# Four 32-column TensorE tiles for the softmax sums and value products of a fused attention and SwiGLU kernel

## The chip, the cores and the metric

The kernel runs on one core of one Trainium2 chip. The metric is the device time of one execution in microseconds (us). A profile of one execution gives the span of the instructions on the core, which is a little shorter than the time of the run.

## The reference

Eight batches of eight heads, 576 positions, 64 channels: causal attention over a sliding window of 64 positions. Its result, with the heads side by side (512 features for each of 4608 tokens), goes through a SwiGLU block with 1536 hidden features.

```python
scores = scale * np.matmul(q, k.transpose(0, 1, 3, 2))
mask = (rel >= 0) & (rel < window)          # window = 64
scores = np.where(mask, scores, -1000000000.0)
attn = np.exp(scores - np.max(scores, axis=-1, keepdims=True))
attn = attn / (np.sum(attn, axis=-1, keepdims=True) + 1e-09)
attn_out = np.matmul(attn, v)
...
x = attn_out.transpose(0, 2, 1, 3).reshape(B * S, H * D)
g = x @ w_gate
out = (g / (1.0 + np.exp(-g)) * (x @ w_val)) @ w_out
```

## The kernel before

The 4608 tokens are worked in nine groups `t` of 512. Groups 0 to 6 and group 8 are the first 512 positions of one batch each; group `LAST` (7) holds the last 64 positions of all eight batches. Within a group everything lies transposed: features on the 128 partitions, the 512 tokens along the free dimension. Heads are taken in four pairs `u`; head `2u` uses partitions 0 to 63 and head `2u+1` partitions 64 to 127.

For one group, `scores(t, u)` multiplies keys and queries block by block on 64x64 tiles of TensorE, ScalarE (ACT) takes the exponential of a two-bank PSUM tile into the weights `E`, and from group 1 on VectorE (DVE) multiplies `E` with a mask. Keys lie on the partitions of `E`, 128 of them as two blocks of 64. `totals` (L251) multiplies `E` with ones to get the softmax sums, copied onto the 64 partitions of each head: one 512-column matmul per head on a 128x64 tile. ACT takes the logarithm of the sums (`log`, L259) and the exponential of its negative (`invert`, L262), which gives the inverse. `mix` (L275) multiplies the values with `E`: for each of eight 64-token blocks `m` and each head of the pair one matmul of 64 stationary columns (the channels of `v1` or of `v2`, a copy of `v1` shifted by 64 positions) and 64 moving columns. `scale` (L285) multiplies the result by the inverse into `xT`, chunk `u` of four. PSUM tiles for scores, wide sums and products come from `ps_a` (two tiles of two banks); those for gates, outputs and single sums from `ps_f` (tags `g` and `v`, two banks each).

Then come twelve `gate_value` steps `m` (L332), each with four matmuls of `xT` with `wg` and four with `wv`, a Silu on ACT (L325) and a product on DVE (L326) into `hT`. `project` (L341) multiplies `hT` with `wo`, twelve matmuls for each quarter `s` of the group's tokens; its output is copied by `project_end` and stored.

The order on each engine is that of the program text; nothing is rescheduled. From group 2 on a group's attention runs between the four projections of the group before: scores of pairs 0 and 1, `project(t-1, 0)`, scores of pairs 2 and 3, sums of pairs 0 and 1, `project` 1 and 2, sums of pairs 2 and 3, all products (`mix_all`), `project(t-1, 3)`, and then the twelve gate steps, in which the next group's queries and keys are turned by DVE.

The start is written out by hand. Queries, keys and half the values of group 0 come over the SP and ACT queues as float32; they are cast by ACT, DVE and POOL (GpSimd) as the table `casts` says (L450) and turned on TensorE (`turn_pe`). Filler matmuls (`keep_warm`, L411) stand between. POOL issues, in this order, the other half of the values of group 0, `wg` and `wv` in column ranges (`weights_gv`, L166), the keys of group 1 (`k_r`, L73), the last range of `wg` and `wv`, the queries of group 1 (`q_s`, L87), two thirds of `wo` (L172), the values of group 1 (L128) and the last third of `wo`. POOL's issue of a transfer waits, with eight under way, for the one eight issues back to land. Gate steps 0 and 1 of group 0 are interleaved with the products of pairs 2 and 3 (`gate_part`, L312). During gate steps 5 to 9 the keys of group 1 are joined by ACT and turned on TensorE (L180); DVE turns its queries (`turn_q`, L192) from step 9 on. Group 0's projection is done for all four quarters at once, in chunks `columns(c0, c1)` of `hT` between group 1's scores, sums and products.

Of the kernel before, what the change touches and what calls it, by code (L numbers as in the profile page):

```python
# [17 lines left out]
def kernel(  # L18
# [131 lines left out]
    def shift_pair(t, u):  # L150
        hs = slice(2 * u, 2 * u + 2)
        a, b = v1[t % 2][:, :, hs], v2[t % 2][:, :, hs]
        nc.vector.tensor_copy(b[64:128, 1:4], a[64:128, 0:3])
        nc.vector.tensor_copy(b[0:64], a[0:64])
# [9 lines left out]
    def weights_gv(f0, f1, c0=0, c1=4):  # L164
        for src, dst in ((moe_w_gate, wg), (moe_w_val, wv)):
            nc.gpsimd.dma_start(  # L166
                dst[:, c0:c1, f0:f1],
                src[P * c0:P * c1, f0:f1].rearrange("(c r) f -> r c f", r=P),
            )
# [79 lines left out]
    def totals(t, u, d_ps):  # L249
        for h in range(2):  # L250
            nc.tensor.matmul(  # L251
                d_ps[64 * h:64 * h + 64], ones[:, 0:D], weights[t, u][:, h, :]
            )
# [10 lines left out]
    def sums(t, u, d_ps):  # L264
        totals(t, u, d_ps)
        r = room(1)[:, 0]
        log(r, d_ps)
        invert(r)
        inverse[t, u] = r

    def mix(t, u, o_ps):
        E = weights.pop((t, u))
        for m in range(8):
            for h in range(2):
                nc.tensor.matmul(  # L275
                    blocks(o_ps[64 * h:64 * h + 64], t, m, m + 1),
                    (v1, v2)[m // 4][t % 2][:, m % 4, 2 * u + h, :] if t == LAST
                    else (v2, v1)[m % 2][t % 2][:, m // 2, 2 * u + h, :],
                    blocks(E[:, h, :], t, m, m + 1),
                )  # L280

    def scale(t, u, o_ps):
        if u == 0:
            xT[t] = att.tile([P, 4, 512], BF16, name="xT", tag="xT")
        nc.vector.tensor_mul(xT[t][:, u, :], o_ps, inverse.pop((t, u)))  # L285

    def values(t, u, o_ps):
        mix(t, u, o_ps)
        scale(t, u, o_ps)

    def wide(name):
        return ps_a.tile([P, 2, 512], FP32, name=name, tag="a")
# [4 lines left out]
    def finish_values(t):  # L297
        for u in (2, 3):
            sums(t, u, d_tile())
        mix_all(t)  # L300

    def mix_all(t):
        tiles = wide("ao_ps"), wide("ao_ps")
        for u in range(4):
            mix(t, u, tiles[u // 2][:, u % 2])
        for u in range(4):
            scale(t, u, tiles[u // 2][:, u % 2])
# [144 lines left out]
    def one(name):  # L452
        return ps_a.tile([P, 2, 512], FP32, name=name, tag="a")[:, 0]

    casts = ((on_a, on_v), (on_p, on_a), (on_a, on_p), (on_v, on_a))
# [15 lines left out]
    cast_first(1, 1)  # L471
    load_v(nc.gpsimd, v1[0], 0, (2, 3))
# [3 lines left out]
    cast_first(2, 0)  # L476
# [7 lines left out]
    weights_gv(0, 256, 0, 2)  # L484
    weights_gv(0, 256, 2, 4)
# [8 lines left out]
    load_qk(1)  # L494
    weights_o(0, 4)
    weights_o(4, 8)
    load_v(nc.gpsimd, v1[1], 1)
    weights_o(8, 12)
# [3 lines left out]
    d_ps, r = wide("d_ps"), room(2)  # L502
    for u in range(2):
        totals(0, u, d_ps[:, u])
        inverse[0, u] = r[:, u]
    log(r, d_ps[:])
    invert(r)
    scores(0, 3)

    def log_of(u):  # L510
        d_ps = one("d_ps")
        totals(0, u, d_ps)
        inverse[0, u] = room(1)[:, 0]
        log(inverse[0, u], d_ps)

    keep_warm(2)
    log_of(2)
    for u in range(2):
        shift_pair(0, u)
    for u in range(2):  # L520
        values(0, u, ps_f.tile([P, 512], FP32, name="ao_ps", tag="gv"[u])[:])
    for u in (2, 3):
        shift_pair(0, u)
    log_of(3)
    for u in (2, 3):
        invert(inverse[0, u])
    keep_warm(1)
    pairs = [gate_tiles() for _ in range(2)]
    for c in range(2):
        gate_part(0, (0, 1), pairs, c)  # L530
    for u in (2, 3):
        values(0, u, one("ao_ps"))
    for c in range(2, 4):
        gate_part(0, (0, 1), pairs, c)
    set_silu()
    for m in range(12):
# [11 lines left out]
        if 5 <= m < 9:  # L548
            u = m - 5
            join(on_a, keys[:, u], raw_k[:, 2 * u:2 * u + 2])  # L550
        if 6 <= m < 10:
            u = m - 6
            tp = ps_a.tile([P, 512], BF16, name="tp", tag="a")
            transposes(tp, keys[:, u])
            split_k(kT[1][:, u, :], tp[:])
        if m >= 9:
            turn_q(1, m - 9)
    turn_q(1, 3)
# [6 lines left out]

    for u in range(4):
        scores(1, u)
        if u == 1:
            columns(0, 4)
    columns(4, 7)  # L570
    for u in (0, 2):
        d_ps, r = wide("d_ps"), room(2)
        for i in range(2):
            totals(1, u + i, d_ps[:, i])
            inverse[1, u + i] = r[:, i]
        log(r, d_ps[:])
        invert(r)
    load_qk(2)
    load_v(nc.gpsimd, v1[0], 2)
    for u in range(4):  # L580
        shift_pair(1, u)
    columns(7, 10)
# [5 lines left out]
    for t in range(1, NT):  # L588
        if t > 1:
# [5 lines left out]
            for u in range(2):  # L595
                sums(t, u, d_tile())
            for s in (1, 2):
                project(t - 1, s)
            finish_values(t)
# [61 lines left out]
```

## Time and profile before

| | before |
|---|---|
| time, median of 3 runs | 333.24 us (332.94 to 333.24) |
| profiled execution: span of the core | 331.9 us |
| PE busy (matmul) | 324.5 us |
| PEld busy (weight loads) | 154.6 us |
| DVE busy | 211.3 us |
| ACT busy | 168.6 us |
| POOL busy | 139.8 us |
| mean DMA rate | 131 GB/s |

The page gives busy time and count of instructions for each engine; matmuls are pipelined, so a row's mean length (379 ns for a 512-column matmul) is longer than the step from one to the next. A line such as "`L341 PE MATMUL o_ps<-wo,hT`" names the line of the kernel, the engine, the operation, the tile written and the tiles read. A bracket at the end of a timeline row gives the engine's idle time before the row and what ended it. The chain of waits follows the work that ended last back from the end, and names at each step what released it.

### The profile page before, as it was taken

The page shows a single profiled execution, that of the slowest core. Times are in us where ns is not written, and L with a number is a line of the kernel's source. Part 1 is how long each engine was busy: PE and PEld are TensorE (multiplying, and loading weights), DVE is VectorE, ACT ScalarE, POOL GpSimd, SP SyncE. Part 2 cuts the span into 40 slices and gives each one's busy share as a digit, 9 for nine tenths or more (in the row PEclk, how much of TensorE's full clock was granted, in tenths as well). Part 3 has the DMA queues.
Part 4 walks back from the last instruction along what each step waited for, and adds up shares of the span by engine and source line. Part 5 has one row for each costly group of instructions (what it writes and reads, how often), then busy time and mean ns, then how long its engine had stood idle before and what let it go on. Part 6 is the DMA issues. An engine that isn't in the chain of part 4 may idle for free.

```text
span 331.9 us, 6997 instructions
## 1 busy us (share of the span) xinstructions
PE 324.5 (98%) x2743; PEld 154.6 (47%) x2743; DVE 211.3 (64%) x325; ACT 168.6 (51%) x239; POOL 139.8 (42%) x249
## 2 busy tenths in 40 slices
PE   8899999999999999999999999999999999999995
PEld 4444444444544454445444444444444544454443
DVE  5855756586576856875668566856785586754431
ACT  5855556338533853377336743565347533953310
POOL 4944535846848985457024986263200000000000
PEclk9999999999999999999999999999999999999998
DMA  7999999999999779859922999199401320010013
GB/s 258 188 196 202 203 190 201 152 192 219 185 236 179 89 136 253 140 80 218 191 58 32 171 203 140 17 199 181 97 0 41 89 55 2 24 73 33 2 34 95
DMA packets 83249, 43.59 MB, mean 131 GB/s; under 512 B 63888, under 2 KB 77968, under 8 KB 83216
## 3 DMA queue, kind: packets, MB, share of 16 engines
q0 software_dynamic: 50416, 23.08, 56.4%
q1 hardware_dynamic: 31776, 19.02, 21.0%
q10 hardware_dynamic: 1024, 1.05, 1.1%
q8 instruction: 21, 0.34, 0.4%
q14 instruction: 12, 0.10, 0.1%
HBM read 54.00 MB, written 9.44 MB: 191 GB/s over the span
## 4 chain that ended last, share of the span: by engine, by line
PE 87%; DMA 8%; POOL 3%; issue 0%; SPq 0%; DVE 0%; POOLq 0%
PE o_ps L341 28%; PE g_ps L332 25%; PE v_ps L332 25%; DMA k_r<-in_k_dram 4%; DMA wo<-in_moe_w_out_dram 3%; PE s_ps L233 3%; PE d_ps L251 3%; PE ao_ps L275 2%; DMA q_f<-in_q_dram 1%; POOL wg L166 1%; POOL wv L166 1%; PE o_ps L377 1%; POOL v L128 1%; POOL qk_b L450 0%; SPq L73 0%
## 5 line engine op out<-in xcount | busy, mean ns | idle before, releaser
L325 ACT ACTIVATE sg<-g_ps 128x512 f32<-128x512 f32 x108 | 64.4, 597 | 116.4 <-PE g_ps L332 87.7
L326 DVE TENSOR_TENSOR hT<-sg,v_ps 128x512 bf16<-128x512 f32 x108 | 74.7, 693 | 60.7 <-PE v_ps L332 57.0
L332 PE MATMUL g_ps<-xT,wg 128*128 128x512 bf16 x424 | 108.8, 379 | 0.1
L332 PE MATMUL v_ps<-xT,wv 128*128 128x512 bf16 x424 | 108.8, 379 | 0.0
L341 PE MATMUL o_ps<-wo,hT 128*128 128x512 bf16 x420 | 95.2, 380 | 0.1
L107 POOL DMA_DIRECT2D k_s<-in_k_dram x112 | 60.6, 559 | 34.2 <-DMA q_s<-in_q_dram 21.6
L332 PEld LDWEIGHTS <-wv 128*128 128x128 bf16 x424 | 41.5, 98 | 50.0
L332 PEld LDWEIGHTS <-wg 128*128 128x128 bf16 x424 | 41.3, 98 | 49.5 <-issue 0.6
L341 PEld LDWEIGHTS <-hT 128*128 128x128 bf16 x420 | 39.0, 98 | 48.0 <-issue 3.3
L239 ACT ACTIVATE E<-s_ps 128x1024 bf16<-128x1024 f32 x36 | 35.1, 1020 | 8.3 <-PE s_ps L233 8.2
L202 DVE STREAM_TRANSPOSE kT<-k_s 128x512 bf16<-128x512 bf16 x28 | 35.9, 1281 | 0.0
L259 ACT ACTIVATE r<-d_ps 128x512 f32<-128x512 f32 (+1 forms) x33 | 20.8, 629 | 16.8 <-PE d_ps L251 16.7
L241 DVE TENSOR_TENSOR E<-E,mask 128x1024 bf16<-128x1024 bf16 x28 | 19.9, 709 | 12.2 <-ACT E L239 12.2
L285 DVE TENSOR_TENSOR xT<-ao_ps,r 128x512 bf16<-128x512 f32 x36 | 22.5, 684 | 6.8 <-PE ao_ps L275 6.4
L87 POOL DMA_DIRECT2D q_s<-in_q_dram x28 | 15.2, 553 | 23.5 <-DVE qT L192 13.4
L192 DVE STREAM_TRANSPOSE qT<-q_s 128x512 bf16<-128x512 bf16 x32 | 22.4, 703 | 0.9 <-DMA q_s<-in_q_dram 0.9
L262 ACT ACTIVATE r<-r 128x512 f32<-128x512 f32 (+1 forms) x33 | 22.0, 669 | 1.0
L148 POOL CAST v<-v_f 128x512 bf16<-128x512 f32 x20 | 12.4, 636 | 18.3 <-DMA v_f<-in_v_dram 12.8
L233 PE MATMUL s_ps<-qT,kT 64*64 64x128 bf16 (+1 forms) x640 | 12.4, 211 | 0.2
L387 ACT ACT_TABLE_LOAD x9 | 11.5, 1283 | 2.0 <-issue 1.9
L94 POOL DMA_DIRECT2D q_s<-in_q_dram x16 | 8.6, 628 | 9.4 <-DVE qT L192 9.4
L251 PE MATMUL d_ps<-E,ones 128*64 128x512 bf16 x72 | 11.4, 390 | 0.8 <-ACT E L239 0.8
(102 smaller groups left out, 186.9 us busy)
## 6 DMA issues: line engine op xcount, KB each, us to landing
q_s<-in_q_dram POOLq DMA_DIRECT2D x28, 248.0 KB, 7.1
k_s<-in_k_dram POOLq DMA_DIRECT2D x112, 56.0 KB, 5.1
v_f<-in_v_dram SPq DMA_DIRECT2D x22, 256.0 KB
v<-in_v_dram POOLq DMA_DIRECT2D x18, 128.0 KB, 4.8
wo<-in_moe_w_out_dram POOLq DMA_DIRECT2D x3, 512.0 KB, 12.0
v<-v SPq DMA_DIRECT2D x6, 256.0 KB
v<-v SPq DMA_DIRECT2D x6, 192.0 KB
q_f<-in_q_dram SPq DMA_DIRECT2D x4, 256.0 KB
```

The lines of the kernel that those rows point to most:

```text
L107: nc.gpsimd.dma_start(k_s[p0:p0 + 32, g, :, 0:w], k[b, a:H:2, s:s + P].rearrange("u (r e) d -> r u (e d)", e=4) [:, :, 32 * c:32 * c + w],)
L192: nc.vector.transpose(queries[t][:, u, :].rearrange("r (e x) -> r e x", e=16), staged[t][0][:, u].rearrange("r (e d) -> r e d", d=D)[:, :, ...
L202: nc.vector.transpose(dst[:, u, :].rearrange("r (g x e) -> r g e x", g=4, e=4), k_s[:, :, u].rearrange("r g (e d) -> r g e d", d=D)[:, :, ...
L233: nc.tensor.matmul(blocks(s_ps[64 * c:64 * c + 64, h], t, lo, hi), zero[r] if src is None else src[r, u, x:x + 64], blocks(qT[r], t, lo, h ...
L239: nc.scalar.activation(E[:], s_ps[:], AF.Exp, scale=0.125)
L251: nc.tensor.matmul(d_ps[64 * h:64 * h + 64], ones[:, 0:D], weights[t, u][:, h, :])
L262: nc.scalar.activation(r, r, AF.Exp, scale=-1.0)
L285: nc.vector.tensor_mul(xT[t][:, u, :], o_ps, inverse.pop((t, u)))
L325: nc.scalar.activation(sg[:], g_ps[:], AF.Silu)
L326: nc.vector.tensor_mul(hT[t][:, m, :], sg[:], v_ps[:])
L332: nc.tensor.matmul(ps[:], w[:, c, P * m:P * m + P], xT[t][:, c, :], start=(c == 0), stop=(c == 3),)
L341: nc.tensor.matmul(o_ps[:], hT[t][:, c, P * s:P * s + P], wo[:, c, :], start=(c == 0), stop=(c == 11),)
```

## The change

Sums and products no longer run on two 128x64 tiles but on four 128x32 tiles, one for each of four heads, all four writing different 32-partition strips of one PSUM bank. Head pairs give way to halves `b` of four heads. The sums of a half are four matmuls with 32 columns of ones, and one bank of sums (and one logarithm and one inverse) serves four heads. The products of a half are split by the parity `g` of the channel: the stationary operand takes every second channel of a head (`g:D:2`, 32 columns), and the even and odd channels go to two banks, which the same inverse scales. A group has 128 product matmuls instead of 64, each with 64 moving columns, and eight sum matmuls as before.

The features in `xT` so lie in another order, and `weights_gv` loads the rows of `wg` and `wv` to match: partition `p` of a half gets rows `2p` and `2p+1` of 256. Each column range is now loaded in four transfers, two for `wg` and two for `wv`.

The head of the program is rewritten around this. Of the casts, the third pair's queries go to POOL (ahead of the value loads) and its keys to ACT. The shifts of `v` go by halves. The sums of the first half stand before `scores(0, 3)`, those of the second half between the two products; the sixteen gate matmuls of steps 0 and 1 follow in one piece. The keys of group 1 are joined and turned two gate steps later, and its queries after the last gate step. In POOL's queue the queries of group 1 come after two thirds of `wo`, and the last third of `wo` before the values. Chunks 0 to 3 of group 0's projection come before group 1's scores, the others are cut anew. In groups 2 to 8 the order is kept, with one set of sums at each of the two places.

The diff, cut to its core:

```diff
-    def shift_pair(t, u):
-        hs = slice(2 * u, 2 * u + 2)
+    def shift_half(t, b):
+        hs = slice(4 * b, 4 * b + 4)
...
-    def weights_gv(f0, f1, c0=0, c1=4):
-        for src, dst in ((moe_w_gate, wg), (moe_w_val, wv)):
-            nc.gpsimd.dma_start(
-                dst[:, c0:c1, f0:f1],
-                src[P * c0:P * c1, f0:f1].rearrange("(c r) f -> r c f", r=P),
-            )
+    def weights_gv(f0, f1, halves=range(2)):
+        for b in halves:
+            for src, dst in ((moe_w_gate, wg), (moe_w_val, wv)):
+                nc.gpsimd.dma_start(
+                    dst[:, 2 * b:2 * b + 2, f0:f1],
+                    src[256 * b:256 * b + 256, f0:f1].rearrange("(p g) f -> p g f", g=2),
+                )
...
-    def totals(t, u, d_ps):
-        for h in range(2):
+    def totals(t, b, d_ps):
+        for j in range(4):
             nc.tensor.matmul(
-                d_ps[64 * h:64 * h + 64], ones[:, 0:D], weights[t, u][:, h, :]
+                d_ps[32 * j:32 * j + 32], ones[:, 0:32],
+                weights[t, 2 * b + j // 2][:, j % 2, :],
             )
...
-    def mix(t, u, o_ps):
-        E = weights.pop((t, u))
+    def mix(t, b, o_ps):
+        E = [weights.pop((t, 2 * b + i)) for i in range(2)]
         for m in range(8):
-            for h in range(2):
...
+            w, i = (m // 4, m % 4) if t == LAST else (1 - m % 2, m // 2)
+            for g in range(2):
+                for j in range(4):
+                    nc.tensor.matmul(
+                        blocks(o_ps[g][32 * j:32 * j + 32], t, m, m + 1),
+                        (v1, v2)[w][t % 2][:, i, 4 * b + j, g:D:2],
+                        blocks(E[j // 2][:, j % 2, :], t, m, m + 1),
+                    )
...
-        nc.vector.tensor_mul(xT[t][:, u, :], o_ps, inverse.pop((t, u)))
...
+        r = inverse.pop((t, b))
+        for g in range(2):
+            nc.vector.tensor_mul(xT[t][:, 2 * b + g, :], o_ps[g], r)
...
-    casts = ((on_a, on_v), (on_p, on_a), (on_a, on_p), (on_v, on_a))
+    casts = ((on_a, on_v), (on_p, on_a), (on_p, on_a), (on_v, on_a))
...
     cast_first(1, 1)
+    cast_first(2, 0)
     load_v(nc.gpsimd, v1[0], 0, (2, 3))
...
-    load_qk(1)
     weights_o(0, 4)
     weights_o(4, 8)
+    load_qk(1)
+    weights_o(8, 12)
     load_v(nc.gpsimd, v1[1], 1)
-    weights_o(8, 12)
...
+    first_sums = [ps_f.tile([P, 512], FP32, name="d_ps", tag=x)[:] for x in "gv"]
+    log_of(0, 0, first_sums[0])
+    invert(inverse[0, 0])
     scores(0, 3)
...
+    for b in range(2):
+        shift_half(0, b)
     keep_warm(1)
+    tiles = wide("ao_ps"), wide("ao_ps")
+    mix(0, 0, tiles[0])
+    scale(0, 0, tiles[0])
+    log_of(0, 1, first_sums[1])
+    invert(inverse[0, 1])
+    mix(0, 1, tiles[1])
+    scale(0, 1, tiles[1])
     pairs = [gate_tiles() for _ in range(2)]
-    for c in range(2):
-        gate_part(0, (0, 1), pairs, c)
-    for u in (2, 3):
-        values(0, u, one("ao_ps"))
-    for c in range(2, 4):
+    for c in range(4):
         gate_part(0, (0, 1), pairs, c)
...
-        if 5 <= m < 9:
-            u = m - 5
+        if 7 <= m < 11:
+            u = m - 7
             join(on_a, keys[:, u], raw_k[:, 2 * u:2 * u + 2])
-        if 6 <= m < 10:
-            u = m - 6
+        if 8 <= m < 12:
+            u = m - 8
...
-        if m >= 9:
-            turn_q(1, m - 9)
-    turn_q(1, 3)
+    for u in range(4):
+        turn_q(1, u)
...
+    columns(0, 4)
     for u in range(4):
         scores(1, u)
         if u == 1:
-            columns(0, 4)
-    columns(4, 7)
...
+            columns(4, 6)
+    columns(6, 8)
+    d_ps, r = ps_a.tile([P, 2, 512], FP32, name="d_ps", tag="a"), room(2)
+    for b in range(2):
+        totals(1, b, d_ps[:, b])
+        inverse[1, b] = r[:, b]
+    log(r, d_ps[:])
+    invert(r)
     load_qk(2)
     load_v(nc.gpsimd, v1[0], 2)
-    for u in range(4):
-        shift_pair(1, u)
-    columns(7, 10)
+    shift_v(1, nc.vector.tensor_copy)
+    columns(8, 10)
     mix_all(1)
...
-            for u in range(2):
-                sums(t, u, d_tile())
+            sums(t, 0)
             for s in (1, 2):
                 project(t - 1, s)
-            finish_values(t)
+            sums(t, 1)
+            mix_all(t)
             project(t - 1, 3)
```

## The prediction

> **What bounds the kernel now.** I read the busy shares first, then the chain that ended last, then one steady stage of TensorE's timeline, then the head of the kernel on POOL, DVE and PE. From the page, and from the chain in order of time:
>
> ```profile
> span 331.9 us, 6997 instructions
> PE 324.5 (98%) x2743; PEld 154.6 (47%) x2743; DVE 211.3 (64%) x325; ACT 168.6 (51%) x239; POOL 139.8 (42%) x249
> ...
> PE 87%; DMA 8%; POOL 3%; issue 0%; SPq 0%; DVE 0%; POOLq 0%
> ```
>
> ```profile
> 16.40 12.26 DMA k_r<-in_k_dram
> 28.95 11.12 DMA wo<-in_moe_w_out_dram
> 40.12 3.63 PE o_ps L341 x16
> ...
> 53.70 1.02 PE g_ps L332 x4
> ```
>
> So there are two regimes. From 53.70 us on (the gate matmuls of group 1) TensorE alone sets the end; before that a stream of transfers runs beside it, and the chain passes through two of them. A steady group, from TensorE's timeline (start, length in us, then the operation; a row merges neighbours of one kind):
>
> ```profile
> 109.81 2.76 PE L341 MATMUL o_ps<-wo,hT 128*128 128x512 bf16 x12
> ...
> 113.09 0.62 PE L251 MATMUL d_ps<-E,ones 128*64 128x512 bf16 x4
> 113.65 5.35 PE L341 MATMUL o_ps<-wo,hT 128*128 128x512 bf16 x24
> 118.93 0.62 PE L251 MATMUL d_ps<-E,ones 128*64 128x512 bf16 x4
> 119.39 1.18 PE L275 MATMUL ao_ps<-E,v 128*64 128x64 bf16 x64
> 120.50 2.76 PE L341 MATMUL o_ps<-wo,hT 128*128 128x512 bf16 x12
> ```
>
> Here sums and products run two 64-column tiles at once. The single starts inside these rows: two sum matmuls 3 ns apart, the next two 237 ns later; products in pairs 3 to 4 ns apart, and 31.7 ns from pair to pair (119.387 to 120.369 over 31 steps). A 512-column matmul in a stream starts 216 ns after the one before, so 64 columns are 27 ns of streaming: the products are near the streaming limit of their 64 moving columns, not of the 64 stationary ones. Groups 2 to 7 begin their gates 34.7 us apart (88.57, 123.26, 157.96).
>
> The head, from POOL's and DVE's timelines:
>
> ```profile
> 36.63 0.75 POOL L172 DMA_DIRECT2D wo<-in_moe_w_out_dram x1 [0.32 <-DMA q_s<-in_q_dram]
> 38.28 0.55 POOL L87 DMA_DIRECT2D q_s<-in_q_dram x1 [0.90 <-issue]
> 40.36 0.55 POOL L87 DMA_DIRECT2D q_s<-in_q_dram x1 [1.52 <-DMA wo<-in_moe_w_out_dram]
> 42.91 0.54 POOL L87 DMA_DIRECT2D q_s<-in_q_dram x1 [2.00 <-DMA wo<-in_moe_w_out_dram]
> ```
>
> ```profile
> 37.67 0.71 DVE L192 STREAM_TRANSPOSE qT<-q_s 128x512 bf16<-128x512 bf16 x1 [0.89 <-DMA q_s<-in_q_dram]
> ```
>
> POOL's issues wait for the landing of the transfer eight issues back, so these rows give landings: the queries of group 1 (q_s) at about 37.5, the first two thirds of wo at 40.1 and 42.6. The busy-time windows give 201, 207 and 191 GB/s of DMA for the ten-us stretches from 20 to 50 us: the stream is full, and what is moved back in it arrives later.
>
> [...] from the last product's start at 120.369 to the next projection at 120.497 is 128 ns where 32 would do. The change swaps one mode for another and adds no switch. [...]
>
> **The change, part by part.**
>
> *Sums, steady groups.* Before: 8 matmuls in four pairs, 4 x 0.237 us at two places. After: 8 matmuls in two sets of four, so 0.237 us less at each place, if four tiles stream like two. At the first place the second half needs the mask product of weights 1, which on DVE ends at 113.10 (112.34 + 0.76); it can start at about 113.17 instead of 113.09, which gives 0.07 back. Saved: 2 x 0.237 - 0.07 = 0.40 us a group. Bounds: nothing, if the four run as two pairs; 0.47 without the wait.
>
> *Products, steady groups.* Before: 64 matmuls in 32 pairs. After: 128 with 32 stationary columns in 32 sets of four, each still streaming 64 columns. I take 32 x 31.7 ns = 1.01 us as before, hence nothing saved. Bounds: 32 x 27 = 0.87 us (gain 0.14) if the shorter load was what lay between 27 and 31.7; 2.03 us (loss 1.01) if instructions, not columns, set the pace, for 256 loads and matmuls must now pass instead of 128. For the low price: four loads and four matmuls of the scores start within 12 ns at 109.22, and 8 per 31.7 ns is slower than that. But that burst may come from a filled queue; over a whole product stretch the trace shows only 128 in 1.01 us. The weight's step of two elements costs nothing in this estimate.
>
> *ACT and DVE, steady groups.* Two logarithm/inverse pairs (590 and 630 ns) less; ACT waits there, so nothing on the path. The four xT products stay four; they start when one wide bank is full, at half the stretch as before, and hide behind the last 12 projection matmuls (2.7 us). Sums of pairs 2 and 3 end earlier than before relative to the products. Nothing.
>
> Groups 2 to 8: 7 x 0.40 = **2.8 us saved**.
>
> *The head up to 19 us.* ACT loses two 1,024-wide operations for two 512-wide (about 0.9 us) and two more of the halves (about 1.2 us), four large v shifts replace eight, and the first 16 gate matmuls run in one piece instead of around the second products (17.46 to 18.77 us). I get gate matmuls 0 and 1 done near 18.9 instead of 20.5 us. Against it, POOL casts the third q piece before the two v loads, which start some 0.65 us later.
>
> *The weight loads.* wg and wv come in 20 transfers instead of 12, same bytes and same run lengths. POOL takes 0.70 us per issue of 128 KB, the stream about 0.65: for the first 12 the issue is a little slower than the stream. I charge 0.4 us to all that follows; bounds 0 and 1.0. Gate 6 (columns 768 up) then waits some 0.8 us, and gates end near 37.9 us instead of 38.9, including the four transposes that move two gates later. k_r lands near 29 us, the moved casts need it after gate 7 at about 29.9: hidden.
>
> *The order of loads.* q_s of group 1 now comes behind two pieces of wo. The same set of bytes had landed at 42.6 us before; with the 0.4 q_s now lands at **43.0 us** instead of 37.5. In their queue nothing else waits but the last wo (45.6) and v (49.0), needed near 50. Four chunks of the projection are moved ahead of the scores: 16 x 216 ns = 3.5 us, until 41.4. Then PE waits for qT, until 43.0 + 0.17 + 0.70 = 43.9: a new wait of about 2.5 us, with the scores, all further projection chunks and gates 1 behind it in PE's queue.
>
> From q_s's landing to gates 1, by the durations before: first two scores end at +1.9; chunks 4 and 5 +3.8; two scores +4.5; chunks 6 and 7 +6.3; fourth weights (exponential 1.0, mask 0.7) ready at +7.1, sums end +7.4; chunks 8 and 9 +9.2; products +10.3; last chunks +12.1; gates +12.2. So gates 1 start near 43.0 + 12.2 = 55.2 instead of 53.70. Head: **1.5 us lost**, call it 1.4, as group 1's sums may squeeze a little. Bounds: gain 1.0 (the early gain survives) to loss 4.0 (a longer chain, or a fallen clock).
>
> Sum against the profile's own span: 331.9 + 1.4 - 2.8 = 330.5 us. The three timed runs give 333.24 (332.94 to 333.24), the profiled execution 333.77 by that clock, so I apply the difference of -1.4 to 333.24: **331.8 us**. About 0.2%, or 0.67 us, is what a measurement can tell from no change.
>
> **Rivals.**
> - *The head keeps its gain* (0.12): q_s lands by 41 or the wait is shorter, gates 1 start at 52.7 to 53.7. For it: ACT, the early bound, loses 2 us. Against: the byte stream. Then -2.8 - 0.5 on average: 329.9, down to 329.4.
> - *Four tiles are paced by instructions* (0.15), ends slower: a set of four takes up to two pair steps, 63.4 ns. Products 2.03 us in eight groups: 8 x 1.01 = 8.1, so 331.8 + 8.1 = 339.9 us. It decides from 1.4 us / (8 x 32) = 5.5 ns more per set, that is 37 ns. Against it the 12 ns burst.
> - *Four sums do not run at once* (0.08): the 2.8 is absent, the head remains: 334.6.
> - *A worse head* (0.10): [...] q_s lands at 44.5: 1.5 to 3 us more, 333.3 to 334.8.
> - That the change does not do what it says: the pages would still show pairs; included in the third.
>
> **How the numbers follow.** Main case 0.55, own range 331.0 to 332.8, of which 0.45 faster, 0.09 same, 0.01 slower. First rival all faster; fourth half same, half slower; third 0.02 same, 0.06 slower; second slower. Faster 0.57, same 0.16, slower 0.27. The range 329.4 to 335.0 leaves out the instruction-paced case above and a sliver below.
>
> **What would show it.** Right: d_ps in rows of four with 0.3 to 0.4 us each, ao_ps x128 in about 1.0 to 1.2 us, gates 34.3 us apart from group 2 on; the first scores of group 1 released by DVE qT with 2 to 3 us idle near 41 to 44; gates 1 near 55. Wrong: ao_ps rows near 2 us; gates 1 before 54; or d_ps rows still 0.6 us.

## The result and the profile after

The changed kernel is slower: 336.1 us (335.38 to 336.96) against 333.21 (332.94 to 333.24) beside it, a ratio of 1.009 with a 95% interval of 1.0065 to 1.0114. Its profiled execution, the longest of its four, spans 335.0 us where the one before spans 331.9, so 3.1 us are to be found. From its page: the span, the busy time, the granted clock by slices of 8.4 us, the queue that brings instructions (packets, MB, share), and the shares of the chain that ended last:

```profile
span 335.0 us, 8109 instructions
...
PE 323.6 (97%) x3317; PEld 154.9 (46%) x3317; DVE 212.6 (63%) x315; ACT 149.5 (45%) x207; POOL 144.0 (43%) x257
...
PEclk9899979999999999999999999999999999999999
...
q8 instruction: 26, 0.43, 0.5%
...
PE 84%; DMA 9%; POOL 3%; issue 1%; ACT 1%; DVE 1%; SPq 0%; DVEq 0%
```

ACT lost 19 us of work and nothing came of it, since it was not the bound. PE's busy time fell by only 0.9 us while the span grew, so PE stands still more. The clock line has dents in the second and sixth slice that the line before (9 throughout, but for the end) does not have. The instruction queue carries 26 transfers instead of 21, for 574 more matmuls and as many more weight loads. "issue" is 1% of the chain instead of 0%.

The chain of the changed kernel in order of time, then PE's timeline at the place where the chain shows the issue time:

```profile
32.21 11.72 DMA q_s<-in_q_dram
44.81 1.23 PE s_ps L234 x29
46.04 2.91 PE o_ps L340 x8
...
57.38 1.02 PE g_ps L331 x4
...
91.48 1.14 issue
```

```profile
89.15 2.33 PE L340 MATMUL o_ps<-wo,hT 128*128 128x512 bf16 x10
92.62 0.59 PE L340 MATMUL o_ps<-wo,hT 128*128 128x512 bf16 x2 [1.14 <-issue]
93.05 1.02 PE L331 MATMUL g_ps<-xT,wg 128*128 128x512 bf16 x4
```

The chain no longer passes through `wo` before group 1 but through its queries, and gates 1 start at 57.38 us instead of 53.70. Later, in the middle of twelve projection matmuls of one kind, PE stands for 1.14 us and nothing that the profile shows holds it.

A steady group of the changed kernel, PE's timeline:

```profile
117.74 0.42 PE L252 MATMUL d_ps<-E,ones 128*32 128x512 bf16 x4
118.09 5.35 PE L340 MATMUL o_ps<-wo,hT 128*128 128x512 bf16 x24
123.37 0.40 PE L252 MATMUL d_ps<-E,ones 128*32 128x512 bf16 x4
123.60 1.31 PE L281 MATMUL ao_ps<-E,v 128*32 128x64 bf16 x128
124.84 2.76 PE L340 MATMUL o_ps<-wo,hT 128*128 128x512 bf16 x12
```

Read from start to start: the first sums hold PE for 0.33 us (before 0.555; 0.35 in the group shown), the second for 0.227 (before 0.456), the products of groups 2 to 6 with the switch behind them for 1.24 to 1.25 (before 1.112).

The starts of the gates split the 3.0 us by which the last matmul moved (327.68 to 330.64):

| stretch | before, us | after, us | difference |
|---|---|---|---|
| start to gates 1 | 53.70 | 57.38 | +3.68 |
| gates 1 to gates 2 | 34.70 | 35.67 | +0.97 |
| six stretches, gates 2 to gates 8 | 208.28 | 206.59 | -1.69 |

Five of the six save 0.31 to 0.36 each; the last, 34.64 instead of 34.70, saves 0.06.

Last the head, from the changed kernel's PE and DVE timelines:

```profile
38.88 3.75 PE L340 MATMUL o_ps<-wo,hT 128*128 128x512 bf16 x16
44.81 0.26 PE L234 MATMUL s_ps<-qT,zero 64*64 64x64 bf16 x2 [2.17 <-DVE qT L193]
...
45.98 2.97 PE L340 MATMUL o_ps<-wo,hT 128*128 128x512 bf16 x8
...
49.47 1.90 PE L340 MATMUL o_ps<-wo,hT 128*128 128x512 bf16 x8
```

```profile
44.05 2.49 DVE L193 STREAM_TRANSPOSE qT<-q_s 128x512 bf16<-128x512 bf16 x4 [3.82 <-DMA q_s<-in_q_dram]
```

The forecast wait is there: four chunks of the projection, then 2.17 us of nothing until DVE has turned the queries. But the same eight matmuls take 2.97 us right after it and 1.90 us a little later: from 44.77 to 48.18 us the trace has the granted clock at half. It has it at half from 14.05 to 17.46 us too.

### The profile page after: what moved, and what is told of

It reads as the page before. It is cut to its first block, busy times and chain, and to the rows that moved or that the text cites. A ratio compares the mean times of both kernels' runs of the same rounds, so it can differ in the third digit from the quotient of the medians.

```text
span 335.0 us, 8109 instructions
## 1 busy us (share of the span) xinstructions
PE 323.6 (97%) x3317; PEld 154.9 (46%) x3317; DVE 212.6 (63%) x315; ACT 149.5 (45%) x207; POOL 144.0 (43%) x257
## 4 chain that ended last, share of the span: by engine, by line
PE 84%; DMA 9%; POOL 3%; issue 1%; ACT 1%; DVE 1%; SPq 0%; DVEq 0%
PE o_ps L340 27%; PE g_ps L331 25%; PE v_ps L331 25%; DMA q_s<-in_q_dram 3%; PE s_ps L234 3%; PE ao_ps L281 3%; DMA k_r<-in_k_dram 3%; DMA wv<-in_moe_w_val_dram 2%; PE d_ps L252 2%; DMA q_f<-in_q_dram 1%; POOL wv L167 1%; POOL wg L167 1%; PE o_ps L376 1%; POOL v L128 1%; ACT E L240 1%
## 5 line engine op out<-in xcount | busy, mean ns | idle before, releaser
L340 PE MATMUL o_ps<-wo,hT 128*128 128x512 bf16 x420 | 96.7, 383 | 1.1 <-issue 1.1
L240 ACT ACTIVATE E<-s_ps 128x1024 bf16<-128x1024 f32 x36 | 35.1, 1021 | 13.6 <-PE s_ps L234 13.5
L242 DVE TENSOR_TENSOR E<-E,mask 128x1024 bf16<-128x1024 bf16 x28 | 22.0, 793 | 11.6 <-ACT E L240 11.6
L261 ACT ACTIVATE r<-d_ps 128x512 f32<-128x512 f32 (+1 forms) x17 | 10.7, 628 | 24.8 <-PE d_ps L252 24.8
L281 PE MATMUL ao_ps<-E,v 128*32 128x64 bf16 x1152 | 12.8, 202 | 1.1 <-DVE v L154 1.1
L281 PEld LDWEIGHTS <-v 128*32 128x32 bf16 x1152 | 12.1, 98 | 3.2 <-DVE v L154 1.9
```

The lines of the kernel that those rows point to most:

```text
L240: nc.scalar.activation(E[:], s_ps[:], AF.Exp, scale=0.125)
L242: nc.vector.tensor_mul(E[:].rearrange("r h x -> r (h x)"), E[:].rearrange("r h x -> r (h x)"), maskl[:].rearrange("r h e b x -> r (h e b x ...
L281: nc.tensor.matmul(blocks(o_ps[g][32 * j:32 * j + 32], t, m, m + 1), (v1, v2)[w][t % 2][:, i, 4 * b + j, g:D:2], blocks(E[j // 2][:, j % 2 ...
L340: nc.tensor.matmul(o_ps[:], hT[t][:, c, P * s:P * s + P], wo[:, c, :], start=(c == 0), stop=(c == 11),)
```

## The experiments

The theory after the result: (1) the sums gain and the products lose a little; (2) the order of loads makes PE wait, and the wait halves the clock; (3) PE stands still now and then because it runs out of instructions. Rivals: the step of two in the weights, the doubled weight loads, and a product stretch that is too dense. Medians, ranges and ratios to the kernel before on the same chip; the last column tells of one profiled execution, which need not be a typical one:

| kernel | median, us | range | ratio (95%) | profiled: clock halved before gates 1, gates 1 at, still in group |
|---|---|---|---|---|
| changed, again | 335.70 | 334.18 to 336.42 | 1.0061 (1.0039 to 1.0083) | yes, 56.28, 1 to 2 |
| wait filled | 334.47 | 332.81 to 336.23 | 1.0036 (1.0024 to 1.0049) | no, 56.90, 5 to 6 |
| old order of loads | 333.64 | 331.99 to 335.88 | 1.0012 (0.9996 to 1.0028) | no, 54.39, none |
| contiguous channels | 334.79 | 332.87 to 338.22 | 1.0052 (1.0033 to 1.007) | yes, 58.73, 1 to 2 (its longest run; only product rows are compared) |
| sums alone | 330.87 | 330.54 to 331.03 | 0.9925 (0.9905 to 0.9946) | no, 53.13, none |
| products in two bursts | 335.64 | 334.11 to 336.72 | 1.0059 (1.0036 to 1.0082) | yes, 57.3, none |
| single weight loads | 334.95 | 333.00 to 336.82 | 1.0043 (1.0028 to 1.0058) | yes, 56.62, none |
| combined | 332.92 | 331.36 to 335.25 | 0.9983 (0.9969 to 0.9998) | yes, 55.06, none |
| combined, filled | 333.39 | 332.73 to 334.99 | 1.0001 (0.9987 to 1.0016) | no, 53.86, 5 to 6 |
| filled, one burst | 332.36 | 331.47 to 335.34 | 0.9971 (0.9955 to 0.9986) | no, 53.92, 5 to 6 |
| 116 extra instructions | 331.49 | 331.27 to 331.85 | 0.9944 (0.9932 to 0.9957) | no, 53.05, none |
| 28 extra instructions | 332.21 | 331.45 to 332.93 | 0.9966 (0.9953 to 0.9979) | no, 54.60, none |

**Old order of loads.** The queries before `wo` again, scores before the projection's chunks:

```diff
-    weights_o(0, 4)
-    weights_o(4, 8)
     load_qk(1)
-    weights_o(8, 12)
+    weights_o(0, 4)
+    weights_o(4, 8)
     load_v(nc.gpsimd, v1[1], 1)
+    weights_o(8, 12)
...
-    columns(0, 4)
     for u in range(4):
         scores(1, u)
         if u == 1:
-            columns(4, 6)
-    columns(6, 8)
+            columns(0, 4)
+    columns(4, 7)
```

> The changed kernel, with POOL's loads of group 1 back in the order of before (q_s, two pieces of wo, v, last wo) and with the scores of group 1 ahead of the first projection chunks, as before. My theory (the head's 3.7 us come from q_s arriving late, and from the clock that falls in the wait): the scores start at about 39 us, the gates of group 1 at 53.5 to 54.3 instead of 57.4, and the time falls by 3 to 3.7 us, to 332.4 to 333.1. Rival (the head is late because of the doubled weight transfers or the early attention, whatever the order): gates of group 1 after 56, time 335 or more.

PE's timeline of this kernel:

```profile
39.73 0.22 PE L234 MATMUL s_ps<-qT,zero 64*64 64x64 bf16 x2 [1.85 <-DVE qT L193]
...
40.72 3.61 PE L340 MATMUL o_ps<-wo,hT 128*128 128x512 bf16 x16
...
54.39 1.02 PE L331 MATMUL g_ps<-xT,wg 128*128 128x512 bf16 x4
```

The queries land at 38.2 us, PE waits 1.85 us for them, the clock stays full, and gates 1 start at 54.39: 3.0 us earlier than in the changed kernel. The median falls by 2.1 us against the changed kernel's second measurement (1.6 us by the ratios). The order of loads, and what it brings with it, is most of the loss. The runs scatter over 3.9 us, which this theory alone does not explain.

**Wait filled.** The changed kernel with ten matmuls of 512 columns after `columns(0, 4)`, whose result nobody reads:

```diff
     columns(0, 4)
+    hot = ps_a.tile([P, 512], FP32, name="hot", tag="a")
+    for _ in range(10):
+        nc.tensor.matmul(hot[0:D], ones[:, 0:D], ones[:])
```

> The changed kernel, with ten filler matmuls of 512 columns after the first projection chunks, in the wait for q_s; loads and everything else as they are. If the fallen clock (half from 44.8 to 48.2 us) is a cost of its own, the next 32 score matmuls and 8 projection matmuls run at full pace and the gates of group 1 start 1.2 to 1.7 us earlier, near 55.9; time about 334.6. If only the wait counts, the fillers change nothing: gates at 57.4, time 336.1.

PE's timeline of this kernel:

```profile
41.95 2.35 PE L547 MATMUL hot<-ones 128*64 128x512 bf16 x10
45.55 0.22 PE L234 MATMUL s_ps<-qT,zero 64*64 64x64 bf16 x2 [1.26 <-DVE qT L193]
...
46.50 1.90 PE L340 MATMUL o_ps<-wo,hT 128*128 128x512 bf16 x8
...
56.90 1.02 PE L331 MATMUL g_ps<-xT,wg 128*128 128x512 bf16 x4
```

The queries landed still later here (44.7 us), yet the first chunks take 1.90 us instead of 2.97, and from the first scores to gates 1 it is 11.35 us instead of 12.57. So the halved clock cost 1.2 us; the medians say the same (335.70 to 334.47; by the ratios 0.8 us). The rest of the profile is not typical: it is the longest of the kernel's 22 executions.

**Contiguous channels.** Products take channels 0 to 31 and 32 to 63 instead of even and odd:

```diff
-    (v1, v2)[w][t % 2][:, i, 4 * b + j, g:D:2],
+    (v1, v2)[w][t % 2][:, i, 4 * b + j, 32 * g:32 * g + 32],
```

> The changed kernel, with the stationary channels of a product taken as 32 neighbours instead of every second one (the channels then meet the wrong weight rows, so it is another computation; same instructions, shapes and transfers). If the step of two is what makes a set of four products take 35 ns instead of 32, the product stretch falls from 1.13 to about 1.01 us and the time by 9 x 0.12 = 1.1 us, to 335.0. If the number of instructions or of tiles is the cause, nothing changes: 1.13 us and 336.1.

The channels then meet the wrong weight rows, so this is another computation with the same instructions. Its product stretch in the group shown above:

```profile
124.69 1.31 PE L281 MATMUL ao_ps<-E,v 128*32 128x64 bf16 x128
```

From first to last start it is 1.119 to 1.120 us, and 1.118 to 1.131 with every second channel. The step of two is not what slows the products.

**Sums alone.** The kernel before, with four sums on four tiles in groups 2 to 8 and nothing else. Each head's inverse then lies on 32 partitions and its products on 64, so the result is not the one asked for; the shapes are:

```diff
-            for u in range(2):
-                sums(t, u, d_tile())
+            sums4(t, 0)
...
-        for u in (2, 3):
-            sums(t, u, d_tile())
+        sums4(t, 2)
         mix_all(t)
...
+    def sums4(t, u):
+        d_ps = d_tile()
+        for j in range(4):
+            nc.tensor.matmul(d_ps[32 * j:32 * j + 32], ones[:, 0:32],
+                             weights[t, u + j // 2][:, j % 2, :])
```

> The kernel before, with only the sums of groups 2 to 8 on four 32-column tiles, four heads to a bank and one logarithm and inverse for them (products and loads as before; the inverses then meet the wrong heads, so it is another computation). My term: two times 0.237 us less per group, a little of it lost to the wait for the second mask product, so gates 34.25 to 34.30 us apart instead of 34.70 and the time 333.2 - 7 x 0.42 = 330.3. Rival (four sums stream no faster than two pairs, and something else shortened the groups): 34.70 and 333.2.

PE's timeline of this kernel:

```profile
117.86 0.40 PE L274 MATMUL d_ps<-E,ones 128*32 128x512 bf16 x4
118.19 1.20 PE L287 MATMUL ao_ps<-E,v 128*64 128x64 bf16 x64
119.32 2.76 PE L352 MATMUL o_ps<-wo,hT 128*128 128x512 bf16 x12
```

The second sums hold PE for 0.33 us here, 0.10 more than in the changed kernel: here products on 128x64 tiles follow them, there products on the sums' own 128x32. The groups still come 34.37 us apart, as in the changed kernel: sums and products hold PE for 0.33 + 0.33 + 1.135 = 1.80 us here, 0.33 + 0.227 + 1.243 = 1.80 there, 2.12 in the kernel before. Seven groups of 0.32 are 2.2 us, and the median is 2.4 below that of the kernel before. The whole steady gain is the sums'. Splitting the products loses 0.13 and saves the 0.10 of the switch between tile shapes.

**Changed kernel again.** Unchanged, beside the next three.

> The changed kernel once more, unaltered, as the measure for the others of this call. Both theories: its first runs gave 336.1; the run with neighbouring channels, which has the same instructions, gave 334.8. I expect 334.5 to 336.2, the runs spread over 3 us or more. If TensorE sometimes stands still for about 1.5 us between two matmuls of group 1 or another group (in the profile of the changed kernel at 91.1 us, right after a fetch of instructions had begun at 90.4), the profile shows one or more such gaps.

The queries landed at 43.0 us and gates 1 started at 56.28, with the clock halved from 43.48 to 46.89; at 90.0 two projection matmuls started 0.92 us apart, at the same place of the program as in its first profile. Every part of the loss is there, each of another size. One more is new: the first sums of group 3 took 0.84 us instead of 0.33, as the mask products of DVE, 2.13 us for two instead of 1.64, came late.

**Products in two bursts.** In groups 2 to 8 each half's sums and products go behind a projection of their own:

```diff
-            sums(t, 0)
-            for s in (1, 2):
-                project(t - 1, s)
-            sums(t, 1)
-            mix_all(t)
+            for b in range(2):
+                project(t - 1, b + 1)
+                sums(t, b)
+                ao = wide("ao_ps")
+                mix(t, b, ao)
+                scale(t, b, ao)
             project(t - 1, 3)
```

> The changed kernel, with the products of groups 2 to 8 in two bursts of 64 matmuls instead of one of 128: projection 1, sums and products of the first four heads, projection 2, sums and products of the last four, projection 3. Theory A (256 loads and matmuls in 1.1 us outrun the supply of instructions: sets of four slow from 30 to 35 ns, and now and then TensorE stands still for a fetch): each burst takes 0.50 to 0.56 us, no gap of 1 us or more in the profile, runs within 1.5 us of each other, time 0.7 to 1.5 us under the unaltered one. Rival B (the slow sets and the gaps come from something else, such as four tiles writing one bank): sets at 35 ns and gaps as before, one more change of tiling per group, time 0.5 us above.

PE's timeline of this kernel:

```profile
119.36 0.71 PE L281 MATMUL ao_ps<-E,v 128*32 128x64 bf16 x64
120.01 2.76 PE L340 MATMUL o_ps<-wo,hT 128*128 128x512 bf16 x11
...
122.93 0.75 PE L281 MATMUL ao_ps<-E,v 128*32 128x64 bf16 x64
```

A set of four steps 33 to 34 ns on average in the bursts of 16 sets, 35 in the stretch of 32. Still the groups come 34.45 us apart instead of 34.37; by my estimate from the 0.10 us of a switch between tile shapes, the additional one in each group takes back more than the shorter steps give. No standstill is in this profile, and still the median is that of the changed kernel: the head was as bad (57.3). So the bursts are no remedy for the time.

**Single weight loads.** Old order of loads and scores, as in the first experiment, and from the second column range on one transfer for all rows, as in the kernel before. The rows of those ranges then do not match the features.

```diff
+        if len(halves) == 2 and f0:
+            for src, dst in ((moe_w_gate, wg), (moe_w_val, wv)):
+                nc.gpsimd.dma_start(
+                    dst[:, :, f0:f1], src[:, f0:f1].rearrange("(c r) f -> r c f", r=P))
+            return
```

> The kernel of the first experiment (loads of group 1 in the old order, scores ahead of the projection chunks), with wg and wv from column 256 on in one transfer each per range, rows laid out as before (the rows then do not match the channels, so it is another computation; same bytes, eight transfers fewer). If the doubled transfers delay all that follows, q_s lands 0.5 to 1.0 us earlier, near 37.4, the gates of group 1 start near 53.7 instead of 54.4 and the time falls by 0.7. If the lateness of q_s is only scatter, nothing changes.

The queries land at 38.0 us, 38.2 with the doubled transfers. Five later kernels with doubled transfers and this order have them at 36.9 to 38.2, so no cost of the doubling shows. The median is 1.3 us above that of the old order with doubled loads (1.0 by the ratios), the wrong way; in its profile the clock was halved twice (14.27 and 41.58), in the other's not at all.

**Combined.** Old order of loads and scores, two bursts, and the two loads of `v` ahead of POOL's third cast:

```diff
-    cast_first(2, 0)
     load_v(nc.gpsimd, v1[0], 0, (2, 3))
+    cast_first(2, 0)
```

> Order of loads and of scores as in the first experiment, products in two bursts, and the two v loads of group 0 ahead of POOL's cast of the third q piece; four-tile sums and products as in the change. Theory: head within 0.7 us of the kernel before (gates of group 1 at 53.7 to 54.4), groups 34.35 us apart (0.33 to 0.35 less), no fetch gaps: 333.2 + 0.5 - 7 x 0.34 = 331.3, faster than both. Rival (the tiles themselves cost more than their rows show): 333 or more.

PE's timeline of this kernel:

```profile
39.23 0.22 PE L234 MATMUL s_ps<-qT,zero 64*64 64x64 bf16 x2 [1.85 <-DVE qT L193]
...
40.68 4.76 PE L340 MATMUL o_ps<-wo,hT 128*128 128x512 bf16 x15 [0.22 <-DMA wo<-in_moe_w_out_dram]
```

The wait is as long as with the old order alone, but here the clock is halved from 39.63 to 43.04: the sixteen matmuls of the projection take 4.76 us (one is missing from the record) instead of 3.61, and gates 1 start at 55.06. The time is a hair under that of the kernel before, 1.6 us above what I expected.

**Combined, filled, and filled with one burst.** The combined kernel with eight matmuls of 512 columns before group 1's scores; and the same with the products of groups 2 to 8 in one stretch:

```diff
+    hot = ps_a.tile([P, 512], FP32, name="hot", tag="a")
+    for _ in range(8):
+        nc.tensor.matmul(hot[0:D], ones[:, 0:D], ones[:])
     for u in range(4):
         scores(1, u)
```

> The combined kernel of the last call (old order of loads and scores, products in two bursts, v loads ahead of the cast) with eight filler matmuls in TensorE's wait for q_s before the first scores of group 1. My theory (what is left of the head's loss, and most of the scatter from run to run, is the clock that falls in that wait): gates of group 1 at 53.6 to 54.0 instead of 55.1, time 331.4 or below, runs within 1 us of each other apart from a few. Rival (the scatter is in the arrival of q_s): median 332.9 as without fillers, spread 3 us or more.

> The same as the one beside it, with the products of groups 2 to 8 in one burst of 128 matmuls again, as in the change. Theory: groups 34.37 us apart instead of 34.45, which is 7 x 0.08 = 0.6 us less, against a fetch gap of 0.7 to 1.5 us in group 1 or another in part of the runs: median 330.8 to 331.8, more scatter than its neighbour. Rival (the fetch gaps are frequent and dear): 1 us slower than its neighbour.

The clock stays full in both and gates 1 start at 53.9. Both missed all the same. The first has a higher median than the kernel without fillers (333.39 after 332.92), so here the fillers did not pay; in its profile PE stood still before gates 6, which may or may not be so in its other executions. The second, at 332.36, lies above its range and 1.0 us under its neighbour. Its PE timeline at that place:

```profile
221.94 1.31 PE L281 MATMUL ao_ps<-E,v 128*32 128x64 bf16 x128
223.18 0.61 PE L340 MATMUL o_ps<-wo,hT 128*128 128x512 bf16 x2
224.27 2.32 PE L340 MATMUL o_ps<-wo,hT 128*128 128x512 bf16 x10 [0.48 <-issue]
```

From the start of the last matmul before the standstill to the start of the first one after it are 0.86 us here and 1.72 in the kernel with two bursts, where 0.216 is usual; both come two matmuls after the products.

**Extra instructions.** The 26 instruction transfers of the changed kernel bring 16,384 bytes each, and its program has 6634 loads and matmuls on PE, 255 to a transfer. If instructions are brought in blocks of about that number, then a few more in the head move the blocks' borders in all that follows. The filled kernel with one burst, its fillers replaced by four of 512 and 54 of 16 columns (116 loads and matmuls instead of 16), or by eight and six (28):

```diff
-    for _ in range(8):
+    for _ in range(4):
         nc.tensor.matmul(hot[0:D], ones[:, 0:D], ones[:])
+    for i in range(54):
+        half = slice(64 * (i % 2), 64 * (i % 2) + 64)
+        nc.tensor.matmul(hot[half, 0:16], ones[:, 0:D], ones[:, 0:16])
```

> The filled kernel with one burst, with TensorE's program lengthened by 116 loads and matmuls in the wait for q_s instead of 16 (4 fillers of 512 columns and 54 of 16 columns, about as long together). My theory of the gaps: [...] the gaps seen so far stood at places 1982 and 4798 of the program, a multiple of 256 apart, and a block that holds little but products is used up before the next has come. With 116 more, no block ends within 31 instructions of the end of a product stretch: no gap in any group, the last group 34.4 us like the others instead of 34.6, median 331.2 to 331.6, nine runs in ten within 1 us. Rival (the gaps fall at random): as with 16 more, 332.4 with a tail to 335.

> The same, with TensorE's program lengthened by 28 (8 fillers of 512 columns and 6 of 16): now a block ends 8 instructions before or after the end of the products in groups 2, 6 and 8. Theory: gaps of 1 to 3 us inside or just after the products of those three groups, in most runs, median 333.5 to 337. Rival (position does not matter): as with 16 more, 332.4.

With 116, PE's timeline:

```profile
37.85 1.00 PE L549 MATMUL hot<-ones 128*64 128x16 bf16 x51
38.88 0.22 PE L234 MATMUL s_ps<-qT,zero 64*64 64x64 bf16 x2
...
53.05 1.02 PE L331 MATMUL g_ps<-xT,wg 128*128 128x512 bf16 x4
```

No wait before the scores, no halved clock, no standstill after gates 1, and five runs within 0.6 us. Of the 1.3 us by which its profiled span (329.6 us) is under the filled kernel's (330.9), 0.87 are gates 1 and the rest is the standstill between gates 5 and 6. It is faster than the kernel before and the changed one; its interval overlaps that of the sums alone, whose median is lower and whose edit is far smaller, but which do not give the right result. The last group, expected to shorten, stayed at 34.64. With 28 I had expected standstills in groups 2, 6 and 8 and 333.5 us or more; there were none, and 332.21 is near the rival's 332.4. Two matmuls of the head's projection started 1.3 us apart at 48.33, but there the profile names `wo`; the same wait, 0.3 to 0.5 us of idle PE, stands in the profiles of old order and of the two filled kernels. So the place in the program alone does not decide.

## Why the prediction was wrong

The term that failed is the head's: 1.5 us of loss were forecast and 3.7 came, because the queries landed later and because a wait of about 2.5 us was taken as harmless to the clock. A second loss, PE standing still with nothing in the profile to wait for, was no term of the sum. The groups saved 2.0 us instead of 2.8.

**Sums: right in size, one charge too many.** The saving is 0.224 + 0.229 = 0.45 us a group, from 2 x 0.237. The 0.07 for the mask was hardly there: 0.02 in group 3, nothing in the other groups. It is a matter of the single execution, for in two other profiles with these sums it was 0.5 (changed, again) and 0.36 us (contiguous channels) in group 3. Four column tiles ran at once as two did before (3 ns apart, the next pair 237 ns later): the four sums of the second set start within 10 ns, and PE goes on 227 ns after the first.

**Products: priced at nothing, cost 0.13.** The step "32 x 31.7 ns as before" failed; it was near the low end of the bounds. A set of four steps 31 to 33 ns on average over the first eight sets of a stretch, as much as a pair before, and 36 to 40 over the last eight of groups 2 to 7, where the matmuls start one by one, 7 to 10 ns apart; the mean is 35. That tail fits the rival "paced by instructions", at an eighth of its price (0.13 of 1.01 us) and under its deciding point of 37 ns. It is not shown: that four tiles write one bank, for one, was left untested. The 12 ns burst of the scores spoke against it, but a short burst says nothing of a long stretch, as the prediction itself had noted. Together 0.32 us a group instead of 0.40.

One reading under this step was wrong as well. The prediction put the 31.7 ns of a pair near the streaming of its 64 moving columns. The short fillers of the kernel with 116 extra instructions are pairs on two such tiles with 16 moving columns, and they step 31.6 ns too (22 steps). So the moving columns do not set the pace of a pair. Nor does the count of instructions alone, for in the first eight sets of four twice as many pass in the same time. A pair and a set both load 128 stationary columns; whether that holds them, no run here tells.

**Early gain, weight loads.** Gate steps 0 and 1 were to end near 18.9 us; in the profile of the changed kernel they ended near 20.5, as before. This term was right and the clock hid it: the products waited until 14.34 for the copies of `v`, and from 14.05 to 17.46 the clock was at half. In the ten other profiles of this head without a halved clock there, they end at 18.4 to 19.1. It gains nothing where PE then waits for the queries all the longer. The 0.4 us for the doubled transfers is not borne out by the experiment.

**Landing of the queries: 43.9, not 43.0.** In the four other profiles with this order of loads they landed at 43.0, 43.6, 44.7 and 44.9; 43.0 was the early end. What the 2 us of scatter come from I did not find.

**From the landing to gates 1: the chain was right, the clock was not.** In the filled kernel it is 56.90 - 44.7 = 12.2 us, forecast 12.2. In the changed kernel it is 57.38 - 43.9 = 13.5, and in the three others with this order and a halved clock 13.3 to 13.9. The excess of the head, 3.68 - 1.5 = 2.2 us, is the 0.9 of the landing and these 1.3. The failing step is the one that charged a wait of about 2.5 us nothing for the clock. In all profiles every half-clock stretch before the last matmul is 3.413 us long, and two in one execution start 30.72 us (changed kernel) and 27.31 us (single weight loads) apart, nine and eight times that length; the full-clock stretches of the changed kernel last 10.240, 27.307 and 286.720 us, three, eight and 84 times. From these lengths I estimate that the clock changes only at the borders of windows of 3.413 us, on one grid through an execution. I laid this grid over the profiles up to the last group and summed PE's idle time in each window: with 1.85 us or more idle of 3.41 the next one was at half in all six cases (up to 2.92), with 1.26 and less it never was, and from 1.34 to 1.66 it went both ways. The 1.85 us wait of the combined kernel lay in one window (36.2 to 39.6) and the clock was at half in the next; the same wait in the kernel with the old order was cut in two by a border at 38.85, 0.96 and 0.89 us, and nothing followed. The rival "a worse head", at 0.10, is nearest to what happened, and it was underrated because the planned wait was charged nothing for the clock.

With the old order of loads this is also most of the scatter. One halved window lowers the mean clock of a run by 0.005 (3.413 / 2 / 331). Of the 22 runs with the old order, the eight with a clock of 0.998 or more have a median of 333.21 us, eleven with 0.993 to 0.997 have 333.88, three below have 335.66. All ten timed runs of the changed kernel have 0.995 or less; in those with the wait filled, 17 of 22 have at least 0.998. The filled kernels scatter too (332.81 to 336.23 with the wait filled, mostly at full clock), and that the clock does not explain.

**Not foreseen: PE stands still.** The stretch from gates 1 to gates 2 should have lost 0.32 and gained 0.97: 1.3 us. What fits is the fetching of instructions: one of the 26 transfers began at 90.37 us and took 0.98, and PE went on at 92.62 with nothing else to wait for. The standstills before gates 2 and 6 lie, counted in loads and matmuls of PE's program, at 1982 (three profiles) and 4798 (three, in one of which a DVE product is named as what ended the wait). These are 2816 apart, which at the 255 to a transfer found above is eleven transfers of 256 each. So I estimate a block at 256 loads and matmuls: of projection matmuls it lasts 128 x 0.216 = 27.6 us, and the products of a group use one up in 1.24. In the kernels with 64 product matmuls (kernel before, sums alone) there is no standstill.

The kernel with 28 extra instructions contradicts a rule by place alone, but not one by time. I put borders 256 apart, by this estimate, through every program and matched each with the transfer that must come before it. In the 14 profiles these are 340 pairs. From the start of the transfer to PE's first load behind the border it is never less than 2.20 us; the six standstills end after 2.20 to 2.41, among the eight shortest of the 340 (half are above 11.6). In the two kernels with 64 product matmuls the shortest is 6.4. With 28 extra instructions the transfer for the border at 4798 began just early enough (2.36 us, with no stop), and with 116 it had 2.8. So, with the borders as estimated, PE stood still in these profiles where it came to one within about 2.2 us of the transfer's start. A kernel that changes nothing but the fetching was not made, and why a transfer begins early or late I did not find.

**Sum.** For the profiles: 1.5 forecast for the head, 0.9 late landing, 1.3 clock, 1.3 standstill, and -2.0 instead of -2.8 for seven groups: 3.0 us. For the medians the standstill need not be in every run: filled, the changed kernel is at +1.2, which is its later gates 1 (+3.2) less 2.0; the halved clock makes that +2.4, and the second measurement gave 335.70 - 333.28 = 2.4. That it meets so closely is in part luck, for the +3.2 is from the longest of the filled kernel's 22 executions. What the first one has beyond that (2.9) is not attributed. Also open is why the last group saves so little: in its product stretch PE pauses, mostly once for 0.17 to 0.20 us, in every kernel with 128 product matmuls in one stretch, and not in those with two bursts. It moves with the products and lies at none of the estimated borders.

## What to carry to other kernels

Sum the idle time of TensorE over the 3.413 us windows of the clock (the grid estimated above), not wait by wait: a wait of 2.17 us in the head cost another 1.2 us behind it. Useless matmuls in it paid for themselves in the changed kernel (335.70 to 334.47) and not in the combined one (332.92 to 333.39), so try them and measure. A finer tiling has to be worth its count of instructions: four tiles gained for 512 moving columns (0.45 us for 8 matmuls) and lost for 64 (0.13 for 128), so the half of such a change that has long streams is the one worth having. The sums alone, as tried here, do not give the right result, and a layout that does was not built. Where 256 loads and matmuls, a block by the estimate above, pass in 1.24 us, look at when the instruction transfer began. And when a transfer is put behind others, take the landings of several runs, not of one profile.

## What the runs showed of the hardware

- Back-to-back weight loads and matmuls on four 128x32 tiles of 64 columns step 31 to 33 ns a set over the first eight sets and 36 to 40 over the last eight of 32 (groups 2 to 7 of the changed kernel), where each matmul starts 7 to 10 ns after the one before.
- Pairs of loads and matmuls on two 128x64 tiles step 31.7 ns with 64 moving columns and 31.6 ns with 16.
- A wait of 1.85 us was followed by 3.413 us at half the clock in one kernel (combined) and by full clock in another (old order of loads). On the grid estimated above it lay in one window in the first, and in two, 0.96 and 0.89 us, in the second.
- In six of the 14 profiles two matmuls of TensorE at the end of an attention stage started 0.9 to 1.7 us apart, in five of them with nothing in the profile to wait for, and only in kernels with 128 product matmuls a group. All six stops end 2.20 to 2.41 us after a transfer of instructions began; in 340 cases no load behind a border, as estimated above, starts sooner than 2.20 us after the start of its transfer.
- Four sums on 128x32 tiles held PE for 0.330 us before products on 128x64 tiles (sums alone) and for 0.227 us before products on 128x32 tiles (changed kernel).
